# Where the maxima, the last queries' maxima and the weight steps stand in an attention pair

## The chip, the cores and the metric

The kernel runs on one core of a Trainium2 chip. The metric is the device time of one execution in microseconds (us). A core has TensorE (PE, matmuls; its weight loads are listed as PEld), VectorE (DVE), ScalarE (ACT), GpSimd (POOL), and SyncE (SP), which issues DMAs here. Matmuls write psum, which VectorE and ScalarE can read.

## The reference

Attention of 8 batches and 8 heads with 1152 keys of 64 dimensions, with the queries averaged in twos to 576, then a feed-forward step on the 4608 resulting tokens of 512 features:

```python
q_pool = q.reshape(B, H, S // 2, 2, D).mean(axis=3)
scores = scale * np.matmul(q_pool, k.transpose(0, 1, 3, 2))
scores = scores - np.max(scores, axis=-1, keepdims=True)
attn = np.exp(scores)
attn = attn / (np.sum(attn, axis=-1, keepdims=True) + 1e-09)
attn_out = np.matmul(attn, v)
x = attn_out.transpose(0, 2, 1, 3).reshape(B * S_pooled, H * D)     # 4608 x 512
h = x @ w_in                                                         # 512 x 2048
out = (h - np.tanh(h)) @ w_out                                       # 2048 x 512
```

All is float32. The row maximum is subtracted before the exponential, so it is needed before the first score tile can be finished.

## The kernel before

**Pairs.** Two heads make a pair; there are 32 pairs (`n_pair`), done one after the other, and after them the feed-forward stage (nine chunks of 512 tokens), which the change does not touch. Within a pair the two heads take the two halves of TensorE's rows, so most matmuls come in twos that start together.

**Three phases of a pair.** `scores` runs for 18 places (`NS`: two halves of 288 queries, nine key tiles of 128 each): eight matmuls (high by high, high by low, low by high, and the negative maxima `m_row` through `sel`) into one psum tile, then an exponential on ScalarE to `p`. GpSimd adds the nine `p` of a half in threes (`add_p`, 12 additions a pair). The value products follow, 18 places of four-column-group matmuls `p` by `v` into `o`, copied out by ScalarE after each half (`pv_out`). `sums` then multiplies GpSimd's sums with ones, which gives the softmax's denominators.

**Maxima.** The maxima of a pair are computed one pair ahead. `max_part(pi, i)` is a unit: for i under 12 two matmuls of 128 queries by 384 keys (high parts only), for i = 12 and 13 the last 64 queries (three matmuls for both units); each has a VectorE reduction to `mx`. `max_row` takes the maximum of `mx`, transposes it and sends it through DRAM into `m_row`.

**The ring.** All psum tiles of the attention stage come from one ring of four (`psum()`), in the order of the program: score tiles, maxima units, `o`, the ones products. A slot is free again when its reader has read it: the exponential, the reduction, or a copy on ScalarE.

**Inputs ahead.** For the pair two further on, at place `NS` (the first place of the value products), `query_sums` adds the two halves of the queries on VectorE and `high` makes rounded copies on ScalarE; at `NS` + 9 `minus_high` makes the negated copy, at `NS` + 16 `low` issues GpSimd's accumulating DMA. `load` (at `NS` + 12) fetches K and Q for the pair three further on; `reciprocals` (VectorE, `NS` + 10) come in every fourth pair.

**Weight steps.** The feed-forward weights are split into high and low parts in the background: 16 blocks of six steps, `begin` (ScalarE), `clamp` (three VectorE operations), `mid`, `high` (also loads the next block), one mask, `low` (also stores the block). Four steps are popped in each pair from pair 2 on, so they last until pair 25.

**Order.** Each engine's order is the order of the program: `InOrder` chains every instruction to the one before on its engine, so all have the line of that helper (L37). Instructions of one engine do not overtake each other; the places are fixed in the table `at`, which `run(pi, place)` empties. A maxima unit for the next pair follows the score tiles with place 1 and 2 of every three; the last queries' units stand behind the ones products.

Of the kernel before, what the change touches and what calls it, by code (L numbers as in the profile page):

```python
# [46 lines left out]
def attention_ffn_kernel(  # L47
# [117 lines left out]
    def hidden(s):  # L165

        mm = [(w, x, c) for w, x in ((0, s.x.h), (0, s.x.l), (1, s.x.h)) for c in range(NP)]
        for k in s.parts:
            for j, (w, x, c) in enumerate(mm):
                pe.matmul(s.h[:, k], wi[s.f][:, w, c], x[:, c, k], start=(j == 0), stop=(j == len(mm) - 1))  # L170
# [7 lines left out]
    def shrink(s, before):  # L178
        t = lambda name, dt=F32: gp.tile([P, 512], dt, name=name)
        all_ = t("g_u"), t("g_t"), t("g_s1"), t("g_s2"), t("g_m", mybir.dt.uint8), s.w  # L180
        s.s1 = all_[2]
        s.g_h = gp.tile([P, 512], F32R, name="g_hi", bufs=LAG + 1)
        s.g_l = gp.tile([P, 512], F32R, name="g_lo", bufs=LAG + 1)
        for k in s.parts:
            shrink_part(s, before, s.h[:, k], *(a[:, k] for a in all_))
            before = None
# [42 lines left out]
    with ExitStack() as actx:  # L229
# [27 lines left out]
        def psum():  # L257
            return ring.tile([P, 2, 512], F32, name="ps")
# [93 lines left out]
        def scores(w, half, kt):  # L352

            ks = slice(SQ + kt * P, SQ + (kt + 1) * P)
            qs = slice(half * HQ, (half + 1) * HQ)
            ps = psum()
            mm = [(w.hi[:, ks], w.hi[:, qs]), (w.hi[:, ks], w.lo[:, qs]), (w.lo[:, ks], w.hi[:, qs]), (sel, w.m[:, qs])]
            for i, (a, b) in enumerate(mm):
                for h in range(2):
                    pe.matmul(ps[:, h, 0:HQ], rows(a, h), rows(b, h), start=(i == 0), stop=(i == 3), skip_group_check=True)  # L360
            p = ppool.tile([P, 2, HQ], F32, name=f"p{kt}")
            act.activation(p, ps[:, :, 0:HQ], AF.Exp, scale=1.0 / 16)
            return p

        def tiled(out, lhs, rhs, i, **kw):
            n = lhs.shape[1]
            pe.matmul(out[i * n:i * n + n], lhs, rhs, skip_group_check=True, tile_position=(0, i * n), **kw)

        def add_p(ps, half, kt):

            k, r = divmod(kt, 3)
            if r == 1:
                ps.sum.append(sp_pool.tile([P, 2, HQ], F32, name=f"sum{half}_{k}"))
                pool.tensor_tensor(ps.sum[k], ps[kt - 1], ps[kt], op=ALU.add)
            elif r == 2:
                pool.tensor_tensor(ps.sum[k], ps.sum[k], ps[kt], op=ALU.add)

        def pv_out(w, half, o):
            if half == 0:
                w.o = op.tile([P, SQ], F32, name="o_s")  # L380
            act.activation(w.o[:, half * HQ:(half + 1) * HQ], o[:, 0, 0:HQ], AF.Copy)
            if half == 1:
                sp.dma_start(x_dram[w.hp, :, w.b * SQ:(w.b + 1) * SQ], w.o)

        def sums(w, ps_p):

            ps = psum()
            for i in range(3):
                for h in range(2):
                    for half in range(2):  # L390
                        tiled(ps[:, 0, 0:HQ], ones, ps_p[half].sum[i][:, h], 2 * h + half, start=(i == 0), stop=(i == 2))
            s = op.tile([P, HQ], F32, name="s_s")
            act.activation(s, ps[:, 0, 0:HQ], AF.Copy)
            sp.dma_start(s_dram[w.b, w.hp].rearrange("h (a n) -> (h a) n", a=2), s[0:P:32])
# [74 lines left out]
        work = []  # L469
# [6 lines left out]
        NS = 2 * KT  # L476

        def add(pi, place, f, *args):
            at.setdefault((pi, place), []).append(lambda: f(*args))

        for pi in range(1, n_pair):
            for i in range(12):
                add(pi - 1, i // 2 * 3 + 1 + i % 2, max_part, pi, i)
            if pi >= 2:
                for i in range(12, 14):
                    add(pi - 2, 2 * NS, max_part, pi, i)
            add(pi - 1, NS - 1, max_row, pi)
        for pi in range(n_pair):
            if pi >= 2:
# [54 lines left out]
        def run(pi, place):  # L544
            while at.get((pi, place)):
                at[pi, place].pop(0)()
# [3 lines left out]
        for pi in range(n_pair):  # L550
            w = pairs[pi]
            ps = [Half(), Half()]
            for place in range(NS):
                half, kt = divmod(place, KT)
                ps[half].append(scores(w, half, kt))
                add_p(ps[half], half, kt)
                run(pi, place)
            n = pi + EARLY - n_pair
            if n == 0:
                c = Chunk(0)  # L560
                steps = [Step(x0[0], f, c) for f in range(NF)]
            if n >= 0:
                hw = psum()
                steps[n].h, steps[n].w = hw[:, 0], hw[:, 1]
                hidden(steps[n])
            for place in range(NS):
                half, kt = divmod(place, KT)
                if place == 1 and n >= 0:
                    shrink(steps[n], steps[n - 1] if n else None)
                if kt == 0:  # L570
                    o = psum()
                for h in range(2):
                    tiled(o[:, 0, 0:HQ], w.v[:, kt, h], ps[half][kt][:, h], h, start=(kt == 0), stop=(kt == KT - 1))
                if kt == KT - 1:
                    pv_out(w, half, o)
                run(pi, NS + place)
                if pi >= 2 and place in (3, 6, 11, 15) and work:
                    work.pop(0)()
            sums(w, ps)
            run(pi, 2 * NS)  # L580
        assert not work and not any(at.values()), (len(work), [a for a in at if at[a]])


# [95 lines left out]
```

## Time and profile before

| | us |
|---|---|
| median of 3 runs | 1605.51 (1605.28 to 1606.35) |
| the profiled execution | 1605.09 |
| its span, first to last instruction | 1603.3 |
| one pair, from value products to value products | 24.10 |
| PE / DVE / ACT / POOL busy | 1575.0 / 1202.0 / 988.1 / 1120.2 |
| granted TensorE clock | 0.998 |

A row of a timeline has the start and the length in us, the engine, the line, the operation, the output and inputs by the program's names, the shape, how often it follows itself, and in brackets the engine's idle time before it and what ended it. Neighbours of one kind are merged, so `x4` can be two maxima matmuls and the first two of a score tile, which bear the same names (`ps<-kq_h`) and differ by their 384 or 288 columns. A row of the table of stretches has the stretch, its length, each engine's busy time and instructions in the order PE, PEld, DVE, ACT, POOL, the clock, the DMA share and GB/s. Matmul ends are modelled; their starts are not. `mx<-ps` is the reduction of a maxima unit, `p<-ps` an exponential, `w_t`, `w_hl`, `w_raw` and `w_off` belong to the weight steps, `rec` to the reciprocals, `raw<-q` is the query sum.

### The profile page before, as it was taken

How to read it: one execution, taken by the hardware profiler on the slowest of the kernel's cores; microseconds unless marked ns; L12 is line 12 of the kernel's file. 1: busy time of each engine (PE TensorE's matmuls, PEld its weight loads, DVE VectorE, ACT ScalarE, POOL GpSimd, SP SyncE). 2: the span in 40 equal slices, each digit the busy share in tenths (PEclk: the TensorE clock that was granted, in tenths of full speed). 3: DMA queues.
4: the chain of work that ended last, by engine and by line, in shares of the span. 5: the costliest groups of instructions: out<-in, count | busy, mean ns of one | idle time of the engine just before them, and what ended most of it. 6: DMA issues, size and time to landing. Idle time of an engine off the chain costs nothing.

```text
span 1603.3 us, 30786 instructions
## 1 busy us (share of the span) xinstructions
PE 1575.0 (98%) x12012; PEld 1221.9 (76%) x12012; DVE 1202.0 (75%) x1590; ACT 988.1 (62%) x1615; POOL 1120.2 (70%) x780
## 2 busy tenths in 40 slices
PE   5999999999999999999998999999999999999998
PEld 4777677777777777677777888888888888888886
DVE  6588788897888888775347777777777777777776
ACT  4676677676676676676635556555655655565654
POOL 3787787787787787786846676666757676766654
PEclk9999999999999999999999999999999999999999
DMA  5547767658576768564180101010010202020000
GB/s 173 173 145 205 227 201 230 209 181 275 155 245 200 236 204 263 166 204 122 50 330 20 66 14 67 9 55 23 8 66 14 66 14 66 14 67 14 27 1 27
DMA packets 84068, 193.59 MB, mean 121 GB/s; under 512 B 12370, under 2 KB 38994, under 8 KB 81874
## 3 DMA queue, kind: packets, MB, share of 16 engines
q1 hardware_dynamic: 79458, 164.20, 29.2%
q0 software_dynamic: 4464, 27.43, 8.8%
q8 instruction: 94, 1.54, 0.4%
q14 instruction: 52, 0.43, 0.1%
HBM read 126.12 MB, written 38.04 MB: 102 GB/s over the span
## 4 chain that ended last, share of the span: by engine, by line
PE 93%; DMA 3%; DVE 2%; ACT 1%; issue 0%; SPq 0%; POOLq 0%; POOL 0%; DVEq 0%; ACTq 0%
PE ps L37 47%; PE ps_h L37 23%; PE ps_o L37 23%; DMA w<-wo_dram 2%; DVE mx L37 1%; DMA s_dram<-s_s 0%; DMA rec<-s_dram 0%; DMA x_r<-r_dram 0%; DMA q<-in_q_dram 0%; ACT p L37 0%; DVE ps_w L37 0%; SPq L37 0%; ACT kq_h L37 0%; DVE w_t L37 0%; DVE kq_l L37 0%
## 5 line engine op out<-in xcount | busy, mean ns | idle before, releaser
L37 DVE TENSOR_REDUCE mx<-ps 128x2 f32<-128x768 f32 x448 | 395.5, 925 | 109.5 <-PE ps L37 109.3
L37 ACT ACTIVATE p<-ps 128x576 f32<-128x576 f32 x576 | 353.4, 653 | 84.7 <-PE ps L37 57.7
L37 POOL TENSOR_SCALAR g_m<-g_u 128x512 uint8<-128x512 f32 (+1 forms) x145 | 251.7, 1736 | 194.4 <-ACT g_u L37 181.3
L37 POOL TENSOR_TENSOR sum<-p,p 128x576 f32<-128x576 f32 x192 | 281.4, 1466 | 138.1 <-ACT p L37 138.1
L37 POOL TENSOR_TENSOR sum<-sum,p 128x576 f32<-128x576 f32 x192 | 298.6, 1555 | 15.6 <-ACT p L37 0.6
L37 PE MATMUL ps<-kq_h 64*128 64x288 f32 (+1 forms) x1920 | 284.7, 341 | 10.0 <-ACT kq_h L37 7.6
L37 PE MATMUL ps<-p,v 128*64 128x288 f32 x2304 | 286.4, 407 | 0.0
L37 PEld LDWEIGHTS ps<-p,v 128*64 128x64 f32 x2304 | 162.7, 137 | 114.6 <-ACT p L37 6.1
L37 POOL TENSOR_TENSOR g_lo<-g_s,g_hi 128x512 fp32r<-128x512 f32 (+1 forms) x145 | 186.9, 1289 | 84.7 <-ACT g_hi L37 84.7
L37 PE MATMUL ps_o<-w,g_hi 128*128 128x512 f32 x792 | 244.7, 390 | 1.0 <-ACT g_hi L37 1.0
L37 ACT ACTIVATE g_u<-ps_h 128x512 f32<-128x512 f32 (+1 forms) x142 | 84.1, 592 | 239.6 <-PE ps_h L37 237.9
L37 PEld LDWEIGHTS ps<-kq_h 64*128 64x128 f32 x1920 | 180.5, 185 | 58.7 <-ACT p L37 20.9
L37 PE MATMUL ps_h<-x_h,w 128*128 128x512 f32 (+1 forms) x800 | 216.0, 392 | 4.4 <-DVE g_t L37 4.4
L37 DVE SCALAR_TENSOR_TENSOR ps_w<-g_u,ps_h 128x512 f32<-128x512 f32 (+1 forms) x142 | 98.3, 693 | 162.1 <-ACT g_t L37 161.9
L37 ACT ACTIVATE g_s<-g_u,pc 128x512 f32<-128x512 f32 x290 | 193.2, 714 | 11.3
L37 PEld LDWEIGHTS ps_h<-x_h,w 128*128 128x128 f32 x800 | 150.3, 189 | 37.5 <-DVE g_t L37 4.9
L37 PEld LDWEIGHTS ps_o<-w,g_hi 128*128 128x128 f32 x792 | 148.5, 188 | 33.4 <-ACT g_hi L37 1.4
L37 PE MATMUL ps<-kq_h,kq_l 64*128 64x288 f32 x1152 | 170.3, 292 | 0.0
L37 PE MATMUL ps<-kq_l,kq_h 64*128 64x288 f32 x1152 | 170.3, 292 | 0.0
L37 PE MATMUL ps<-m_row,sel 64*128 64x288 f32 x1152 | 169.5, 291 | 0.0
L37 PE MATMUL ps_o<-w,g_lo 128*128 128x512 f32 x396 | 154.8, 391 | 0.6 <-POOL g_lo L37 0.5
L37 DVE COPY_PREDICATED g_s<-g_m,g_t 128x512 f32<-128x512 uint8 (+1 forms) x145 | 110.0, 758 | 17.0 <-POOL g_m L37 2.1
(112 smaller groups left out, 2359.2 us busy)
## 6 DMA issues: line engine op xcount, KB each, us to landing
kq_l<-raw POOLq DMA_DIRECT2D x31, 864.0 KB, 10.6
raw<-in_k_dram SPq DMA_DIRECT2D x32, 576.0 KB
q<-in_q_dram SPq DMA_DIRECT2D x32, 576.0 KB
v<-in_v_dram SPq DMA_DIRECT2D x32, 576.0 KB
x_dram<-o_s SPq DMA_DIRECT2D x32, 288.0 KB
x_l<-x_dram SPq DMA_DIRECT2D x9, 1024.0 KB
out_dram<-o_f SPq DMA_DIRECT2D x36, 256.0 KB
w_raw<-in_w_in_dram SPq DMA_DIRECT2D x8, 1024.0 KB
```

Source lines behind the costliest of these rows:

```text
L37: i = f(*args, **kwargs)
```

## The change

Three things move; no instruction is added or removed. A place of -1 is new: it runs before a pair's first score tile.

- Maxima units 0 and 1 run at place -1, units 2 to 9 after places 1, 3, ... 15, units 10 and 11 both after place 17, the last. Before, unit i ran after place `i // 2 * 3 + 1 + i % 2`: 1, 2, 4, 5, ... 16, 17.
- Units 12 and 13 run after the last value product (`2 * NS - 1`) and so ahead of `sums`, instead of behind it.
- Weight steps are popped at value places 0, 2, 4 and 6 and ahead of what `run` does there, instead of at 3, 6, 11 and 15 and behind it.

```diff
         for pi in range(1, n_pair):
             for i in range(12):
-                add(pi - 1, i // 2 * 3 + 1 + i % 2, max_part, pi, i)
+                add(pi - 1, min(max(2 * i - 3, -1), NS - 1), max_part, pi, i)
             if pi >= 2:
                 for i in range(12, 14):
-                    add(pi - 2, 2 * NS, max_part, pi, i)
+                    add(pi - 2, 2 * NS - 1, max_part, pi, i)
             add(pi - 1, NS - 1, max_row, pi)
@@
             ps = [Half(), Half()]
+            run(pi, -1)
             for place in range(NS):
@@
                 if kt == KT - 1:
                     pv_out(w, half, o)
+                if pi >= 2 and place in (0, 2, 4, 6) and work:
+                    work.pop(0)()
                 run(pi, NS + place)
-                if pi >= 2 and place in (3, 6, 11, 15) and work:
-                    work.pop(0)()
             sums(w, ps)
-            run(pi, 2 * NS)
```

## The prediction

> **What bounds the kernel now.** I read the page first, then a table of four stretches of one pair each, then the timelines of TensorE, its weight loads, VectorE, ScalarE and GpSimd over one pair.
>
> ```profile
> span 1603.3 us, 30786 instructions
> ...
> PE 93%; DMA 3%; DVE 2%; ACT 1%; issue 0%; SPq 0%; POOLq 0%; POOL 0%; DVEq 0%; ACTq 0%
> ```
>
> ```profile
> 402.67:426.77 24.10, 24.10 (x270) 17.78 (x268) 20.21 (x24) 17.18 (x27) 19.39 (x14) 1.00 0.62 173
> 426.77:450.86 24.09, 24.09 (x270) 17.76 (x268) 21.64 (x25) 16.01 (x26) 19.68 (x14) 1.00 0.68 203
> 669.15:693.25 24.10, 24.10 (x269) 17.74 (x267) 16.38 (x21) 16.41 (x26) 18.59 (x14) 1.00 0.47 138
> ```
>
> TensorE holds the chain, and a pair of heads takes 24.10 us whether VectorE is busy 21.6 us of it (weight steps) or 16.4 us (none). So today no weight step reaches the chain. "Busy" hides short stalls, because matmul ends are modelled; starts do not. Times below count from 402.67 (T), the start of this pair's value products, and from 411.55 (Z = T + 8.88), where they give way to the next kind of matmul.
>
> ```profile
> 402.67 8.95 PE L37 MATMUL ps<-p,v 128*64 128x288 f32 x72
> 411.55 1.66 PE L37 MATMUL ps<-sum,ones 128*32 128x288 f32 x24
> 413.14 0.79 PE L37 MATMUL ps<-kq_h,q_last 128*128 128x384 f32 x3
> 413.86 0.40 PE L37 MATMUL ps<-kq_h 64*128 64x288 f32 x2
> ...
> 415.02 0.65 PE L37 MATMUL ps<-kq_h 64*128 64x384 f32 x4
> ...
> 421.45 0.51 PE L37 MATMUL ps<-kq_h 64*128 64x384 f32 x4
> ...
> 422.21 0.62 PE L37 MATMUL ps<-kq_h 64*128 64x384 f32 x4
> ...
> 423.06 0.30 PE L37 MATMUL ps<-kq_h 64*128 64x288 f32 x2
> ...
> 423.60 0.51 PE L37 MATMUL ps<-kq_h 64*128 64x384 f32 x4
> ...
> 426.50 0.34 PE L37 MATMUL ps<-kq_h 64*128 64x384 f32 x2
> 426.77 0.46 PE L37 MATMUL ps<-p,v 128*64 128x288 f32 x2
> ```
>
> ```profile
> 415.26 0.19 PEld L37 LDWEIGHTS ps<-kq_h 64*128 64x128 f32 x2 [0.19 <-DVE mx L37]
> ...
> 422.43 0.19 PEld L37 LDWEIGHTS ps<-kq_h 64*128 64x128 f32 x2 [0.17 <-ACT p L37]
> ```
>
> A score tile alone takes 0.54 us (423.06 to 423.60), a maxima unit with a tile 0.76 (421.45 to 422.21) or, with the wait at 422.43, 0.85 (422.21 to 423.06). Three tiles and two units repeat every 2.15 us; without that wait 2.03 to 2.06. The wait is the psum ring: four slots handed out in turn, so each tile or unit needs the slot of the fourth allocation before it. At 422.43 that is a tile whose exponential ended just then; at 415.26, the third tile, it is the last-query unit, whose VectorE reduction ended just then. From 415.26 to the next value products is 11.51 us.
>
> **The score phase.** Now the order is two units, then (two tiles, one unit) eight times, two tiles, two units. Per two tiles and a unit the rows give 0.76 + 0.54 = 1.30, of which the 0.76 still contains a few hundredths of waiting. The loop through the reduction is near that:
>
> ```profile
> 402.03 1.82 DVE L37 TENSOR_REDUCE mx<-ps 128x2 f32<-128x768 f32 x2 [0.33 <-PE ps L37]
> ...
> 404.39 1.13 DVE L37 TENSOR_TENSOR raw<-q 128x576 f32<-128x576 f32 x1
> 405.45 1.90 DVE L37 TENSOR_SCALAR w_t<-w_hl 128x1024 int32<-128x1024 int32 x1
> 407.39 2.32 DVE L37 SCALAR_TENSOR_TENSOR w_hl<-w_hl,w_t 128x1024 fp32r<-128x1024 int32 x1
> 410.94 2.15 DVE L37 TENSOR_SCALAR w_t<-w_t 128x1024 f32<-128x1024 f32 x3 [1.23 <-ACT w_t L37]
> 413.79 1.42 DVE L37 TENSOR_REDUCE mx<-ps 128x2 f32<-128x768 f32 x2 [0.70 <-PE ps L37]
> ...
> 421.83 1.82 DVE L37 TENSOR_REDUCE mx<-ps 128x2 f32<-128x768 f32 x2 [0.33 <-PE ps L37]
> ```
>
> A unit at 421.45 is reduced from 421.83 (0.38 later); two reductions take 1.82, one 0.96; the slot is used 0.05 after. 0.38 + 0.96 + 0.05 = 1.39 after a unit the next pair of tiles may load weights, wanted about 1.28 to 1.38 after it. I take 1.29. From the third tile on: 0.63 (a tile after a wait, 422.43 to 423.06) + 0.54 + 7 x 1.29 + 0.17 + 0.27 (the two last units, 426.50 to 426.77 the one) = 10.64 us, instead of 11.51: **0.87 us less**.
>
> **The front of it.** Moving the last queries' three matmuls ahead of the ones products changes no TensorE work: 0.72 (413.14 to 413.86) + 1.59 (411.55 to 413.14) in either order, 2.31 after Z. Then the two new units, at Z + 2.31 and Z + 2.48, and two tiles. The slots: the third tile now needs the second front unit's slot. Its reduction ends 0.38 + 1.82 after Z + 2.31, so the third tile loads at Z + 4.56; today it does at 415.26 = Z + 3.71. **0.85 us more**. TensorE could have been there at 2.31 + 0.17 + 0.17 + 0.57 + 0.53 + 0.18 = Z + 3.93, so 0.63 of this is a new stall. Where VectorE is free, the two parts cancel: 8.88 + 4.56 + 10.64 = 24.08 us, 0.02 below 24.10.
>
> **VectorE in front of it.** Four reductions (last-query pair, two front units) must now be through before the third tile, and they stand behind the weight steps. If VectorE's weight work ends E after Z, they end E + 0.79 + 0.46 + 0.87 + 0.95 (back to back, from 1.42 and 1.82 a pair) and the third tile comes at Z + E + 3.12. It is late from E = 1.44 on, and a pair costs E - 1.46 more than today. Today the first of them is wanted only at 413.79 = Z + 2.24, and only one gates the tile. So what covered the weight steps shrinks by most of a microsecond. In front of them also comes more: both last units now end the phase, so the two reductions end at T + 1.77 (first unit 0.44 before T, 0.38, 1.82) instead of 403.85 = T + 1.18, and all VectorE work up to the next idle time shifts by 0.59.
>
> ```profile
> 405.56 1.64 ACT L37 ACTIVATE kq_h<-raw 128x1728 fp32r<-128x1728 f32 x1 [2.25 <-DVE raw L37]
> ...
> 409.74 1.17 ACT L37 ACTIVATE w_t<-w_raw 128x1024 f32<-128x1024 f32 x1
> ```
>
> ```profile
> 403.51 1.40 POOL L37 TENSOR_TENSOR sum<-p,p 128x576 f32<-128x576 f32 x1
> 404.99 1.81 POOL L37 TENSOR_TENSOR sum<-sum,p 128x576 f32<-128x576 f32 x1
> ...
> 416.04 1.43 POOL L37 TENSOR_TENSOR sum<-p,p 128x576 f32<-128x576 f32 x1 [4.24 <-ACT p L37]
> ```
>
> ```profile
> 457.03 2.83 DVE L37 TENSOR_SCALAR w_t<-w_t 128x1024 f32<-128x1024 f32 x3 [3.31 <-ACT w_t L37]
> ...
> 460.44 1.20 DVE L37 SCALAR_TENSOR_TENSOR w_hl<-w_raw,w_t 128x1024 int32<-128x1024 int32 x1
> ```
>
> ```profile
> 431.38 2.43 DVE L37 SCALAR_TENSOR_TENSOR w_hl<-w_raw,w_t 128x1024 int32<-128x1024 int32 x1
> 433.73 1.38 DVE L37 TENSOR_SCALAR rec<-rec 128x36 f32<-128x36 f32 x1
> 435.14 0.38 DVE L37 RECIPROCAL rec<-rec 128x36 f32<-128x36 f32 x1
> ...
> 436.14 1.22 DVE L37 SCALAR_TENSOR_TENSOR w_hl<-w_hl,w_t 128x1024 fp32r<-128x1024 int32 x1
> ```
>
> The six steps of a block fall four to a pair, so the pairs 2 to 25 come in three kinds, eight of each. The engines run their queues in order, and a step starts when its inputs are there, so other places change only what a step stands ahead of: VectorE's query sum, and ScalarE's copies.
>
> - Kind A (mask, low, begin, clamp; the pair at 402.67). Mask, query sum and low are the same three in another order and end at 409.71 + 0.59 = T + 7.63. Then ScalarE's begin (1.17) and the three clamp operations (2.15), with 0.05 at each hand-over: T + 11.0, E = 2.16. Cost 0.70. Begin now stands ahead of the half's output copy and the minus-high copy (about 1.65, as 405.56); the ring wants the second output copy only at Z + 2.3, so I put that at nothing, at most 0.3.
> - Kind B (mid, high, mask, low; at 426.77). Its last step ends at 437.36 = T + 10.59, with the reciprocals' two operations in front, of which the first (1.38) is mostly a wait; without them about 0.55 less. 10.04 + 0.59: E = 1.8. Cost 0.34.
> - Kind C (begin, clamp, mid, high; at 450.86). VectorE idled 3.31 here, because begin stood behind the high copies. Now begin is ahead of them; the clamp starts after the query sum at T + 3.4. But there GpSimd is still summing, and beside it one such operation takes 1.90 (405.45) instead of 2.15 / 3 = 0.72. 3.4 + 3 x 1.90 + 0.73 + 1.20 = T + 11.0: E = 2.1. Cost 0.64.
>
> Six of the 24 (every fourth pair from 4 on) also hold the reciprocals, 0.55 each that was covered until Z + 2.24. Sum: 8 x (0.70 + 0.34 + 0.64) + 6 x 0.55 - 6 x 0.02 (pairs without weight steps) = 13.4 + 3.3 - 0.1 = **+16.6 us**. The profiled execution took 1605.09 (0.42 below the median 1605.51): 1605.1 + 16.6 = 1621.7, so **1622**.
>
> On kind C one page speaks against the change more strongly than my row. A row shows 1.90 for an operation of 0.72 beside a sum of 1.40. The Trainium skill, "SBUF — State Buffer", Who interferes with whom, holds that the two engines share a port pair under an exclusive lock for a whole instruction, and the second one "fully blocks"; an operation could then wait out a whole sum, 0.72 + 1.40 = 2.12. By the row kind C costs 0.64, by the rule 3 x 0.22 = 0.66 more, and the sum would be 1627.
>
> **Bounds of what I can't see.** E: at best nothing shifts and kind C uses its idle time (E at or under 1.46 everywhere, total -0.6 us); at worst GpSimd's sums, which now start closer to the value products, block one more operation in each kind (+0.5 each, +12 us). The two last units at the end: the value products' first slot is a tile two allocations further back whose exponential has 0.9 us; taken as nothing, at most 0.2 a pair. SyncE: the block's stores and loads now go out ahead of the next K and Q loads.
>
> ```profile
> 437.11 8.89 SPq L37 DMA_DIRECT2D wi_dram<-w_hl  x2
> ```
>
> ```profile
> 446.00:456.00 10.00, 10.00 (x108) 7.29 (x106) 7.00 (x10) 7.04 (x12) 9.77 (x7) 1.00 0.94 319
> ```
>
> Behind such a store the K and Q loads (1.18 MB, 3.7 us at 319 GB/s) go out near 446 instead of before it, and VectorE wants them at 450.86 + 2.3 = 453.2. Some 3 us are left: taken as nothing, at worst 2 us in each kind-B pair. GpSimd's DMA waits for the minus-high copy, up to 2 us later in kind A; the 4.24 us idle at 416.04 hide it.
>
> **Rivals.**
> - *VectorE is in time.* The weight steps, popped earlier, are through by Z + 1.46, as kind C's idle 3.31 allows and kind B (24.09 us, 21.64 busy) speaks against. Then 30 pairs gain 0.02: 1604.5; not slower, no change. 20%.
> - *The third tile does not wait.* If the ring gives it another slot than the second front unit's, the 0.63 stall goes, with VectorE in time 30 x 0.69 (0.06 after the wait too): 1604.5 - 20.7 = 1584. Against it: 415.26 waits for exactly the allocation four back. 12%.
> - *The reduction loop closes each period.* Where weights must be loaded 0.11 before I allow, each of 8 periods stalls 0.11: 30 x 0.88 = 26 us on top, 1648; alone 1631. 10%.
>
> **How the numbers follow.** My forecast has 58%. 0.2% is 3.2 us, about what can be told from no change. Low end: 1604.5 less some 3 for the small terms, 1601; high end: 1622 + 12 (E at worst), 1634; outside are the second rival and most of the third. Faster: 12% and 6% of the first rival's edge. Same: 14% of the first rival and 3% of my forecast's low edge. Slower: the other 65%.
>
> **What would show it.** In the changed profile: a weight load of the third tile idle "<-DVE mx" in every pair (right), near 0.6 us where no weight step runs and 1 to 1.5 where one does; no "<-ACT p" waits of weight loads in mid-phase, a period of 1.29; pairs after 669 still 24.1 us, pairs of kinds A and C 24.6 to 24.9. It is wrong if the weight pairs stay at 24.1 (VectorE in time), if all pairs shrink to 23.4 (no front stall), or if waits of GpSimd or DMA show at the pair's border.

## The result, and the profile after

The changed kernel took 1619.81 us (median; 1619.41 to 1620.13), the kernel before 1606.35 beside it (1605.28 to 1606.93): a ratio of 1.0086, with a 95% interval of 1.0074 to 1.0097. It is 13.5 us slower; the forecast was 1622.

From the page of the changed kernel, the span and the shares of the chain of waits:

```profile
span 1617.9 us, 30798 instructions
...
PE 70%; DVE 20%; DMA 6%; issue 1%; SPq 1%; ACT 1%; DVEq 0%; POOLq 0%; POOL 0%; ACTq 0%
```

TensorE had 93% of the chain. Now a fifth of it runs through VectorE, whose busy time grew by 22 us (1202.0 to 1224.4). The table of stretches of the changed kernel, one pair to a row (stretch, length, busy time of PE, PEld, DVE, ACT, POOL, clock, DMA share, GB/s), shows where:

```profile
707.43:731.59 24.16, 23.74 (x270) 17.89 (x268) 16.73 (x21) 16.07 (x27) 18.85 (x14) 1.00 0.75 243
483.44:508.12 24.68, 24.18 (x269) 17.83 (x267) 20.34 (x24) 16.50 (x27) 19.42 (x13) 1.00 0.65 190
508.12:532.50 24.38, 24.12 (x269) 17.86 (x268) 21.29 (x23) 15.42 (x25) 19.43 (x13) 1.00 0.68 191
458.69:483.44 24.75, 24.19 (x269) 17.84 (x267) 20.33 (x24) 16.63 (x27) 18.55 (x13) 1.00 0.75 244
310.56:334.90 24.34, 24.08 (x269) 17.82 (x268) 21.22 (x24) 16.73 (x27) 19.27 (x13) 1.00 0.74 244
```

In this order: a pair without weight steps, kind A, kind B, and two of kind C. Kind C comes in two lengths, which the prediction did not have, and pairs 24 and 25 are longest of all (26.24 and 25.85). The next table takes the starts of the value products of all pairs in both traces and adds up pair lengths; its sum is the whole difference up to pair 31.

| pairs | before | after | more | forecast |
|---|---|---|---|---|
| 0, 1, 26, 27 (no weight steps) | 96.42 | 96.64 | +0.22 | -0.1 |
| kind A, 3 to 21 (7) | 169.29 | 173.23 | +3.9 | +5.5 |
| kind B, 4 to 22 (7) | 168.70 | 171.59 | +2.9 | +3.5 |
| kind C, 2 to 23 (8) | 192.85 | 197.53 | +4.7 | +6.2 |
| 24 (A, reciprocals) | 25.18 | 26.24 | +1.1 | +1.3 |
| 25 (B) | 24.34 | 25.85 | +1.5 | +0.3 |
| 28 to 30 | 77.54 | 77.47 | -0.1 | 0 |
| sum | 754.32 | 768.55 | +14.2 | +16.6 |

(The forecast column regroups the prediction's own terms: the 0.55 of the reciprocals is in pairs 12, 4 and 16, 8 and 20, and 24.) The traced executions differ by 14.9, somewhat more than the medians.

The timeline of TensorE and of its weight loads in the changed kernel, in the pair from 707.43, which has no weight step (Z = 716.32):

```profile
716.32 0.79 PE L37 MATMUL ps<-kq_h,q_last 128*128 128x384 f32 x3
...
718.63 0.76 PE L37 MATMUL ps<-kq_h 64*128 64x384 f32 x6
...
720.99 0.40 PE L37 MATMUL ps<-kq_h 64*128 64x288 f32 x2 [0.42 <-DVE mx L37]
...
722.15 0.47 PE L37 MATMUL ps<-kq_h 64*128 64x384 f32 x4
...
731.07 0.59 PE L37 MATMUL ps<-kq_h 64*128 64x384 f32 x4
```

```profile
720.99 0.19 PEld L37 LDWEIGHTS ps<-kq_h 64*128 64x128 f32 x2 [0.68 <-DVE mx L37]
```

The first front unit starts 2.31 after Z, the third tile loads at Z + 4.67 after 0.68 of waiting for a reduction, and 10.60 later the next value products start. From 722.15 to 731.07 lie seven units, 1.27 us each with their two tiles, with no such wait between them. In a pair with weight steps the reductions come later, and the wait spreads over the second front unit, the first tile and the third; the weight loads of the pair of kind A from 483.44:

```profile
495.32 0.18 PEld L37 LDWEIGHTS ps<-kq_h 64*128 64x128 f32 x2 [0.50 <-DVE mx L37]
495.79 0.19 PEld L37 LDWEIGHTS ps<-kq_h 64*128 64x128 f32 x2 [0.28 <-DVE mx L37]
...
497.52 0.19 PEld L37 LDWEIGHTS ps<-kq_h 64*128 64x128 f32 x2 [0.51 <-DVE mx L37]
```

Together they are 1.29, against the one wait of 0.68 without weight steps. The totals of the waits, before and then after, tell the same: those of weight loads on exponentials have shrunk to a fifth, those on reductions have grown threefold, and VectorE waits for a load of Q seven times instead of once.

```profile
PEld ps L37 <- ACT p L37: 27.5, 149, 0.4
...
PEld ps L37 <- DVE mx L37: 14.1, 40, 2.7
```

```profile
PEld ps L37 <- DVE mx L37: 42.1, 86, 2.7
...
DVE raw L37 <- DMA q<-in_q_dram: 10.8, 7, 4.5
...
PEld ps L37 <- ACT p L37: 5.9, 32, 0.2
```

(us in all, times, longest.)

### The profile page after: what moved, and what is told of

It is laid out like the page before. It is cut to its first block, busy times and chain, and to the rows that moved or that the text cites. A ratio compares the mean times of both kernels' runs of the same rounds, so it can differ in the third digit from the quotient of the medians.

```text
span 1617.9 us, 30798 instructions
## 1 busy us (share of the span) xinstructions
PE 1572.6 (97%) x12012; PEld 1224.7 (76%) x12012; DVE 1224.4 (76%) x1590; ACT 974.4 (60%) x1615; POOL 1121.1 (69%) x780
## 4 chain that ended last, share of the span: by engine, by line
PE 70%; DVE 20%; DMA 6%; issue 1%; SPq 1%; ACT 1%; DVEq 0%; POOLq 0%; POOL 0%; ACTq 0%
PE ps L37 24%; PE ps_h L37 23%; PE ps_o L37 23%; DVE mx L37 8%; DVE w_hl L37 4%; DVE w_t L37 4%; DMA q<-in_q_dram 4%; DVE raw L37 3%; DMA w<-wo_dram 2%; SPq L37 1%; ACT w_t L37 1%; DMA rec<-s_dram 0%; DVE nm L37 0%; DVE rec L37 0%; DVE ps_w L37 0%
## 5 line engine op out<-in xcount | busy, mean ns | idle before, releaser
L37 DVE TENSOR_REDUCE mx<-ps 128x2 f32<-128x768 f32 x448 | 400.8, 924 | 123.6 <-PE ps L37 123.6
L37 ACT ACTIVATE p<-ps 128x576 f32<-128x576 f32 x576 | 343.1, 652 | 77.9 <-PE ps L37 60.5
L37 POOL TENSOR_SCALAR g_m<-g_u 128x512 uint8<-128x512 f32 (+1 forms) x145 | 247.2, 1705 | 193.7 <-ACT g_u L37 180.9
L37 POOL TENSOR_TENSOR sum<-p,p 128x576 f32<-128x576 f32 x192 | 286.2, 1491 | 125.4 <-ACT p L37 125.4
L37 ACT ACTIVATE kq_h<-raw 128x1728 fp32r<-128x1728 f32 (+2 forms) x33 | 52.8, 1601 | 136.9 <-DVE raw L37 134.6
```

The lines of the kernel that those rows point to most:

```text
L37: i = f(*args, **kwargs)
```

## The experiments

Each ratio is against the kernel before, run beside it, with its 95% interval. E is, as in the prediction, the end of VectorE's weight work after Z.

**The three parts, each alone on the kernel before.** First only the new places of the twelve maxima units:

```diff
-                add(pi - 1, i // 2 * 3 + 1 + i % 2, max_part, pi, i)
+                add(pi - 1, min(max(2 * i - 3, -1), NS - 1), max_part, pi, i)
...
+            run(pi, -1)
```

> The kernel before with the maxima units' new places alone; the last queries' units stay behind the ones products, the weight steps at their old places. Theory (third tile waits for the reduction of the second front unit): now four reductions start only after the ones products. The last-query pair is reduced from Z + 2.24, the two front units from Z + 3.57, the second ends at Z + 5.4, so the third tile comes at Z + 5.5 instead of Z + 4.67 as measured in the changed kernel: a pair without weight steps takes 24.16 + 0.83 = 25.0 us, and nearly all 30 pairs alike, since VectorE's weight work (old places, 0.59 later) ends before Z + 2.24 but for kind C (0.25 late): 1606.3 + 30 x 0.9 + 2 = 1635. Rival (weight steps alone make the loss, the front of the score phase costs nothing): 1606 to 1608.

Measured: 1621.03 us, ratio 1.0095 (1.0081 to 1.0109). This alone costs as much as the whole change, but not in the way that was expected: a pair without weight steps takes 24.50, not 25.0, and kinds A and B take 24.49 to 24.61, kind C without reciprocals 24.54 to 24.63. The last queries' reductions now come behind the ones products, and the weight loads and VectorE of the pair from 683.65 show who waits:

```profile
695.79 0.19 PEld L37 LDWEIGHTS ps<-kq_h 64*128 64x128 f32 x2 [0.65 <-DVE mx L37]
...
697.12 0.46 PEld L37 LDWEIGHTS ps<-kq_h 64*128 64x128 f32 x4 [0.24 <-DVE mx L37]
```

```profile
694.78 4.01 DVE L37 TENSOR_REDUCE mx<-ps 128x2 f32<-128x768 f32 x5 [4.14 <-PE ps L37]
```

It is the first tile that waits (0.65), for a last-query reduction. With the prediction's reduction times (0.79 + 0.46 + 0.87 + 0.95) the second front unit is read at 694.78 + 3.07 = 697.85, but the third tile is in the merged row at 697.12 (a unit and a tile), and so loads before that. It did not take the slot four allocations back. In the compiled program's psum addresses it has the first tile's, whose exponential was over; in all other kernels here the slots do go in turn, up to pair 28. The expectation's step that failed is "third tile waits for the reduction of the second front unit".

Next only the last queries:

```diff
-                    add(pi - 2, 2 * NS, max_part, pi, i)
+                    add(pi - 2, 2 * NS - 1, max_part, pi, i)
...
-            run(pi, 2 * NS)
```

> The kernel before with the last queries' units ahead of the ones products, alone. Theory: the third tile's slot is then the ones products', long copied out; it comes at Z + 3.58 instead of Z + 3.71 and without the 0.06 to 0.1 after a wait: a pair without weight steps takes 23.9 to 23.95 us. The second tile now waits for the first last-query reduction, wanted for weight work that ends by Z + 1.8; kinds A (1.54) and B (1.23) do, kind C (1.90) loses 0.1, pairs with reciprocals some 0.4. 30 x -0.17 + 8 x 0.1 + 6 x 0.3 = -2.5 us: 1603.5 to 1604. Rival (VectorE gates every pair as soon as its reductions are wanted ahead of the ones products): slower than before, 1610.

Measured: 1607.41 us, ratio 1.0008 (0.9999 to 1.0017); nothing gained, where 1603.5 to 1604 were expected. A free pair takes 24.12. The third tile no longer waits, but the tile after it does; the weight loads of the free pair from 671.25:

```profile
684.58 0.19 PEld L37 LDWEIGHTS ps<-kq_h 64*128 64x128 f32 x2 [0.21 <-ACT p L37]
```

The wait moved from a reduction to an exponential. I read this so: with units in pairs in mid-phase ScalarE's exponentials pace the phase, and an earlier third tile meets them sooner.

Third only the places of the weight steps:

```diff
+                if pi >= 2 and place in (0, 2, 4, 6) and work:
+                    work.pop(0)()
                 run(pi, NS + place)
-                if pi >= 2 and place in (3, 6, 11, 15) and work:
-                    work.pop(0)()
```

> The kernel before with the weight steps' new places alone. Theory: VectorE's reductions are wanted only at Z + 2.24, and the weight steps end by Z + 2.1 without the 0.59 that the two last units add; nothing is gated: pairs 24.1 us, 1606 within 1.5 us. The query sum of some kind-C pairs waits for the K and Q loads behind the weight DMAs, covered too. Rival (the steps' new order by itself delays the pairs, by ScalarE's copies or the loads): kinds A and C 24.4 or more, 1611 or more.

Measured: 1605.48 us, ratio 0.9998 (0.9989 to 1.0007). Nearly all pairs take 24.10. E is 1.5 in kind A, 1.2 in B, 1.6 in C: the weight work ends late enough to gate the changed front, but the old front covers it.

**The change with the weight steps where they were.** The edit undoes the third part.

> The changed kernel with the weight steps back at their old places; maxima and last queries as changed. Theory (a pair loses E - 1.46 through VectorE, E now from the kernel before's ends plus 0.59): kind A 1.54 + 0.59 = 2.13, B 1.23 + 0.59 = 1.82, C 1.90 + 0.59 = 2.49, so A 24.8, B 24.45, C 25.1; the new places had helped kind C. But the K and Q loads and the x copies at the pairs 24 and 25 stand as before, about 1 us less there. 8 x 0.35 - 2 = 1 us more than the changed kernel: 1620 to 1622. Rival (the new places cause the loss): 1606 to 1608.

Measured: 1623.63 us, ratio 1.0115 (1.0099 to 1.0130), a little beyond what was expected. Kinds A and B are mostly within 0.1 of the changed kernel; kind C without reciprocals takes 25.05 to 25.08 (E 2.45 to 2.49), pair 2, the first with steps, 24.83. So the new places help kind C, as the prediction had it (begin ahead of the high copies), and their help is hidden in the kernel before.

**Less VectorE work.** In the changed kernel the three clamp operations and the mask are left out, so the weights are not split rightly:

```diff
-                    ts(f(self.t), f(self.t), lo_b, hi_b, op0=ALU.max, op1=ALU.min)
-                    ts(self.t, self.t, 0x08000000, 3, op0=ALU.bitwise_xor, op1=ALU.logical_shift_left)
-                    ts(self.t, self.t, 0x7FFFFFFF, None, op0=ALU.bitwise_and)
+                    pass
...
-                    lambda: ts(self.t, self.hl[:, 0], -0x800000, None, op0=ALU.bitwise_and),
+                    lambda: None,
```

> The changed kernel without the clamp's three VectorE operations and the mask operation of each weight block; the weights are then not split rightly, all else is done. Theory: VectorE is through with the remaining weight work by Z + 1.4 in all kinds, so every pair falls back to the 24.16 us of the pairs without weight steps, with some 0.2 left where reciprocals stand and in the pairs 24 and 25, where ScalarE's x copies stand behind VectorE: 1606.3 + 30 x 0.06 + 1.5 = 1609 to 1610, 10 us less than the changed kernel. Rival (the front wait or the places of the maxima make the loss in every pair): 1618 to 1620.

Measured: 1606.40 us, ratio 1.0004 (0.9995 to 1.0013). All pairs of the three kinds take 24.15 to 24.22; only pair 25 is longer (25.03). The loss is the weight steps' lateness, nearly all of it. The front and the ring alone, in all 30 pairs, cost no more than can be told from nothing.

**One front unit instead of two, one last unit.** This was to test the prediction's "two last units" (both reductions behind the last place shift VectorE by 0.59):

```diff
-                add(pi - 1, min(max(2 * i - 3, -1), NS - 1), max_part, pi, i)
+                add(pi - 1, (-1, 1, 2, 4, 6, 7, 9, 11, 12, 14, 16, 17)[i], max_part, pi, i)
```

> The changed kernel with one unit ahead of the scores and one at the end: units after places -1, 1, 2, 4, 6, 7, 9, 11, 12, 14, 16, 17. Theory: the third tile waits for the first front unit, reduced by Z + 3.70, and TensorE comes at Z + 3.76: no front wait. In the phase four groups of three tiles with two units wait 0.12 each, as in the kernel before, where six did. A pair without weight steps: 8.88 + 3.76 + 10.67 + 0.48 = 23.8; weight work ends 0.59 earlier than in the changed kernel, E at most 1.6, and gates no pair without reciprocals (0.3 with). 30 x -0.3 + 6 x 0.3 + 2 (pairs 24, 25) = -5: 1600 to 1602. Rival (the exponentials' chain, not the front, paces the phase, as in the run with the last queries ahead alone): 24.05 to 24.1 a pair, 1605 or more.

Measured: 1607.94 us, ratio 1.0016 (1.0007 to 1.0025). The table of stretches, a free pair and one of kind A (kind B takes 23.9):

```profile
673.03:696.85 23.82, 23.82 (x270) 17.75 (x268) 17.28 (x21) 16.30 (x27) 18.85 (x14) 1.00 0.50 142
476.36:500.58 24.22, 24.09 (x269) 17.78 (x267) 20.64 (x24) 16.73 (x27) 19.41 (x14) 1.00 0.68 200
```

The whole missed (1600 to 1602 were expected), though the free pair came out at 23.82 where 23.8 was expected: this order of the units is worth 0.34 against the changed kernel where VectorE is free. Kind A did not follow. VectorE and GpSimd in that pair of kind A (T = 476.36):

```profile
475.72 1.82 DVE L37 TENSOR_REDUCE mx<-ps 128x2 f32<-128x768 f32 x2 [0.33 <-PE ps L37]
...
478.09 1.50 DVE L37 TENSOR_SCALAR w_t<-w_hl 128x1024 int32<-128x1024 int32 x1
479.51 1.96 DVE L37 TENSOR_TENSOR raw<-q 128x576 f32<-128x576 f32 x1
481.39 2.44 DVE L37 SCALAR_TENSOR_TENSOR w_hl<-w_hl,w_t 128x1024 fp32r<-128x1024 int32 x1
```

```profile
466.09 1.43 POOL L37 TENSOR_TENSOR sum<-p,p 128x576 f32<-128x576 f32 x1 [3.85 <-ACT p L37]
...
477.63 1.41 POOL L37 TENSOR_TENSOR sum<-p,p 128x576 f32<-128x576 f32 x1
```

And the same rows of the changed kernel (T = 483.44):

```profile
483.30 1.82 DVE L37 TENSOR_REDUCE mx<-ps 128x2 f32<-128x768 f32 x2 [0.29 <-PE ps L37]
...
485.66 1.10 DVE L37 TENSOR_SCALAR w_t<-w_hl 128x1024 int32<-128x1024 int32 x1
486.69 1.96 DVE L37 TENSOR_TENSOR raw<-q 128x576 f32<-128x576 f32 x1
488.57 2.44 DVE L37 SCALAR_TENSOR_TENSOR w_hl<-w_hl,w_t 128x1024 fp32r<-128x1024 int32 x1
492.25 2.15 DVE L37 TENSOR_SCALAR w_t<-w_t 128x1024 f32<-128x1024 f32 x3 [1.24 <-ACT w_t L37]
```

```profile
473.27 1.42 POOL L37 TENSOR_TENSOR sum<-p,p 128x576 f32<-128x576 f32 x1 [4.31 <-ACT p L37]
...
484.81 1.40 POOL L37 TENSOR_TENSOR sum<-p,p 128x576 f32<-128x576 f32 x1
```

Read three times from T: the end of the last reduction, the start of GpSimd's ninth addition, and the end of the last of mask, query sum and low.

| kernel | reduction ends | ninth addition starts | last of the three ends | the last two apart |
|---|---|---|---|---|
| before (pair from 402.67) | 1.18 | 0.84 | 7.04 | 6.20 |
| after | 1.68 | 1.37 | 7.57 | 6.20 |
| one front unit | 1.18 | 1.27 | 7.47 | 6.20 |

The weight work keeps its distance to the additions, to the hundredth, and not to the reductions. The same holds beyond these three: in all pairs of kind A from 3 to 21 of seven kernels (these three, the steps alone, the steps moved back, and two further on, with earlier loads and with both last units at the end) the distance is 6.18 to 6.21, while the ninth addition starts anywhere from T + 0.79 to T + 1.64. With the reduction 0.50 earlier than in the changed kernel, low ends only 0.10 earlier: the first operation merely takes longer (1.50 instead of 1.10) and ends, in both, 0.55 after the end of the ninth addition. The shift that the prediction put down to the two last units belongs to GpSimd.

**Half the additions.** The test of that: GpSimd leaves out the second addition of every three exponentials, six of a pair's twelve, so the denominators lack a third of their terms.

```diff
-            elif r == 2:
-                pool.tensor_tensor(ps.sum[k], ps.sum[k], ps[kt], op=ALU.add)
```

> The changed kernel without every third addition on GpSimd (six a pair instead of twelve), so the softmax's denominators lack a third of their terms; all else is done. Revised theory (VectorE's weight steps are late because each waits out one of GpSimd's additions, which now begin closer to the value products; the two last units have nothing to do with it, since with one unit at the end the weight work ended only 0.07 earlier): with the additions over before the value products, VectorE's weight work ends by Z + 1.2 in every kind and all pairs fall to 24.15 to 24.2, the pairs 24 and 25 to 25: 1606 to 1608. Rival (VectorE is late by its own work and by the 0.5 of the two last units): kinds A and B gain little, 24.5 and 24.3, 1613 or more.

Measured: 1605.84 us, ratio 0.9999 (0.9990 to 1.0008). Everything of the change is in this kernel but those additions, and its loss is gone. VectorE in the pair of kind A from 476.04:

```profile
475.90 1.82 DVE L37 TENSOR_REDUCE mx<-ps 128x2 f32<-128x768 f32 x2 [0.28 <-PE ps L37]
...
478.27 0.65 DVE L37 TENSOR_SCALAR w_t<-w_hl 128x1024 int32<-128x1024 int32 x1
478.84 0.75 DVE L37 TENSOR_TENSOR raw<-q 128x576 f32<-128x576 f32 x1
479.50 1.22 DVE L37 SCALAR_TENSOR_TENSOR w_hl<-w_hl,w_t 128x1024 fp32r<-128x1024 int32 x1
482.89 2.15 DVE L37 TENSOR_SCALAR w_t<-w_t 128x1024 f32<-128x1024 f32 x3 [2.17 <-ACT w_t L37]
```

The reductions end as late as in the changed kernel (T + 1.68), but mask, query sum and low take 2.62 together instead of 5.50, and E falls from 2.08 to 0.13. In kinds B and C the weight work even ends 2.2 and 2.1 before Z. All pairs up to 27 take 24.14 to 24.23, 24 and 25 too. So the cause is VectorE's weight work beside GpSimd's additions: there the three operations take 1.7 to 2.6 times as long as here. That the changed order moves the additions toward them is what the three times above show.

**The K and Q loads earlier.** The changed kernel with the loads issued at the second place of the value products, so ahead of the block's stores in SyncE's queue:

```diff
-                add(max(pi - 3, 0), NS + 12 if pi > 2 else 0, load, pi)
+                add(max(pi - 3, 0), NS + 1 if pi > 2 else 0, load, pi)
```

> The changed kernel with the loads of K and Q for the pair three further on issued at value place 1 instead of 12, so ahead of the weight blocks' stores and loads in SyncE's order. Theory: the kind-C pairs whose query sum waits 1.3 us for Q (5, 14, 17 and with reciprocals 8 and 20) fall to the 24.34 of the pairs 11 and 23, where it doesn't wait: 5 x -0.4 = -2 us, 1617.5 to 1618. Rival (the wait on Q is covered by GpSimd's sums anyway): 1619.8, kind C unchanged.

Measured: 1618.61 us, ratio 1.0083 (1.0070 to 1.0097). As a whole this can't be told from the changed kernel (1.0086), but in the trace the long pairs of kind C take 24.37 to 24.43, where the changed kernel has 24.72 to 24.76. What they had waited for, in the changed kernel, on SyncE's queue and on VectorE (T = 458.69):

```profile
442.33 6.64 SPq L37 DMA_DIRECT2D wi_dram<-w_hl  x2
449.07 6.22 SPq L37 DMA_DIRECT2D r_dram<-rec  x1
...
455.81 0.42 SPq L37 DMA_DIRECT2D q<-in_q_dram  x1
```

```profile
462.32 1.27 DVE L37 TENSOR_TENSOR raw<-q 128x576 f32<-128x576 f32 x1 [1.32 <-DMA q<-in_q_dram]
```

The block's loads, its store and here the reciprocals' store go out first. The two stores hold SyncE's queue for 12.9 us, the Q load is issued at 455.81, and VectorE's query sum, with all weight work behind it, waits 1.32 for it. In pair 13 the stores hold the queue for no more than 2.60, and Q for pair 14's query sum is issued 12.75 us ahead of its value products (371.67 and 384.42); the query sum still waits 0.72, with the DMA engines busy all the time (a stretch of pair 13):

```profile
376.00:381.00 5.00, 5.00 (x74) 4.79 (x72) 3.71 (x5) 4.70 (x8) 4.92 (x4) 1.00 1.02 257
```

There, I take it, Q stands behind the block's bytes: two loads and a store of 1 MB each are some 12 us at such a rate. One pair got longer (18: 24.90 instead of 24.68). Its ninth addition starts at T + 1.64 instead of T + 1.37, and the three operations again end 6.2 after it; why the additions came later there is open.

**One front unit, both last units at the end**, to tell whether two ends cost anything by themselves:

```diff
+                add(pi - 1, (-1, 1, 3, 5, 6, 8, 10, 11, 13, 15, 17, 17)[i], max_part, pi, i)
```

> The changed kernel with one unit ahead of the scores and two at the end: units after places -1, 1, 3, 5, 6, 8, 10, 11, 13, 15, 17, 17. Theory: no front wait, two groups of three tiles with two units: 8.88 + 3.76 + 10.67 + 0.24 = 23.6 a pair without weight steps. VectorE is as late as in the changed kernel (E 2.08, 1.76, 1.74 to 2.13) and the third tile follows E by 2.2: kinds A and C 24.1, B 23.75, reciprocals 0.5 more. 8 x (0 - 0.35 - 0.1) + 6 x 0.5 - 6 x 0.5 + 2 = -1.6: 1603 to 1606; the two last units cost what the two groups saved. Rival (the late reductions do not matter once the third tile waits for the first front unit): 23.6 in all kinds, 1592.

Measured: 1607.98 us, ratio 1.0016 (1.0007 to 1.0024). Free pairs 23.70, kind A mostly 24.20 to 24.24, B 23.91 to 23.97. The total is a little above what was expected, but no dearer than with one last unit, so the time of the last reductions does not matter, and the free pair is 0.40 below the kernel before. The weight pairs and 24 and 25 (25.76 and 25.50) take the gain back.

**Fewer additions with the whole sum.** On top of that kernel, the ninth exponential of each half goes to the ones products directly: ten additions a pair instead of twelve, four terms instead of three.

```diff
-            elif r == 2:
+            elif r == 2 and kt < KT - 1:
...
-            for i in range(3):
+            for i in range(4):
...
+                        a = ps_p[half].sum[i] if i < 3 else ps_p[half][KT - 1]
```

> The run with one unit in front and two at the end, and in each half the ninth exponential goes to the ones products by itself: ten GpSimd additions a pair instead of twelve, four more matmuls of the ones products. By the revised theory GpSimd is done some 3 us earlier and VectorE's weight work ends before Z + 1.4, so no pair is gated: 23.70 + 0.24 (four matmuls in four column groups, as the ones products' 0.24 each) = 23.95 in all kinds, the pairs 24 and 25 near 24.5: 1599 to 1601, faster than before. Rival (VectorE late by its own work): kinds A and C 24.2 + 0.24, 1610 or more.

Measured: 1608.77 us, ratio 1.0017 (1.0008 to 1.0026); a miss. As expected, weight steps cost nothing any more: nearly all pairs take 24.19, with and without them. But the new term costs 0.5, twice what was taken. TensorE there:

```profile
486.18 1.66 PE L37 MATMUL ps<-sum,ones 128*32 128x288 f32 x24
487.66 0.67 PE L37 MATMUL ps<-p,ones 128*32 128x288 f32 x8
```

The program's four products are eight matmuls in the trace (the twelve before them are 24), at 1.48 / 24 = 0.06 each.

On top of that kernel, weight steps from pair 0 on, so that they end with pair 23:

```diff
-                if pi >= 2 and place in (0, 2, 4, 6) and work:
+                if place in (0, 2, 4, 6) and work:
```

> The kernel with four terms of the ones products, with the weight steps from pair 0 instead of pair 2 on, so they are over before the pairs 24 and 25, where ScalarE's x copies stand behind VectorE. Theory: these two pairs fall to 23.95 to 24.1, the pairs 0 and 1 stay at 23.95: 0.5 to 1.5 us less than with the steps from pair 2. Rival (the first weight block's data arrive too late for pair 0, or the x copies are late by themselves): the same or slower.

Measured: 1607.97 us, ratio 1.0007 (0.9998 to 1.0016), 0.8 us less than with the steps from pair 2, as expected, though the two intervals overlap. Pairs 24 and 25 go from 24.98 and 24.33 to 24.20 and 24.19. Why these two are long, in the changed kernel's pair 25 (value products end at 666.30): TensorE, ScalarE, VectorE.

```profile
668.50 1.66 PE L37 MATMUL ps<-sum,ones 128*32 128x288 f32 x24 [1.40 <-ACT o_s L37]
```

```profile
667.42 0.63 ACT L37 ACTIVATE x_h<-x_r 128x512 fp32r<-128x512 f32 x1 [2.73 <-DVE x_r L37]
667.96 0.39 ACT L37 ACTIVATE o_s<-ps 128x288 f32<-128x288 f32 x1
```

```profile
666.71 0.68 DVE L37 TENSOR_TENSOR x_r<-x_l,x_r 128x512 f32<-128x512 f32 x1
```

VectorE's product for the feed-forward stage stands behind the weight steps, ScalarE's copy of it stands ahead of the output copy, and the ones products wait 1.40 for the slot that this output copy frees.

**Together.** One front unit with both last units at the end and all twelve additions, the loads at the second value place, and the steps from pair 0.

> The run with one unit in front and two at the end (twelve additions), the K and Q loads at value place 1, and the weight steps from pair 0 on. Theory: 23.70 a pair without weight steps, kinds A 24.2, B 23.95, C 23.95 (its query sum no longer waits for Q; 24.28 before), 0.45 more with reciprocals, no lost time in the pairs 24 and 25: 3.5 us less than the kernel before, 1602.5, at the edge of what can be told. Rival (the loads and the pairs 24 and 25 are not what made the run with one unit in front and two at the end slower than the sum of its pairs): 1606 to 1608.

Measured: 1600.98 us, ratio 0.9962 (0.9949 to 0.9974), so 5.8 us below the kernel before; the changed kernel, in a comparison of its own, is 13.5 above it. Its stretches: a free pair, and kinds A and C (the kinds fall on other pairs here; kind B is like C).

```profile
643.12:666.82 23.70, 23.70 (x270) 17.79 (x268) 16.93 (x21) 16.17 (x27) 18.83 (x13) 1.00 0.47 141
64.72:88.95 24.23, 23.98 (x270) 17.80 (x268) 20.32 (x24) 16.62 (x27) 19.41 (x13) 1.00 0.60 170
...
474.88:498.78 23.90, 23.90 (x270) 17.83 (x268) 21.22 (x24) 16.83 (x27) 19.27 (x14) 1.00 0.77 241
```

Kind C lost its Q wait (24.23 to 24.31 mostly, before these two edits), and pair 24 has no weight steps any more and takes 23.71, like a free pair. Kind A still costs 0.5 more than a free pair (0.7 in two pairs).

## Why the prediction was right, point by point

- **The forecast and its sign: right.** 1622 forecast, 1619.8 measured; of the +16.6 in terms the trace shows +14.2. "VectorE is in time" fell, since weight pairs did not stay at 24.1, and "the reduction loop closes each period" fell, since the period is 1.27.
- **The front: right.** The third tile was put at Z + 4.56 and came at Z + 4.67; the new stall was put at 0.63, and the weight load is idle for 0.68. **The score phase** was put at 10.64 from there and took 10.60. A free pair should have come to 24.08 and takes 24.16; the 0.08 is the 0.11 at the third tile less 0.04.
- **VectorE in front of it: right, with smaller sizes.** E was put at 2.16, 1.8 and 2.1 for kinds A, B and C, and is 2.08, 1.77 and 1.74, or 2.14 where Q is late. The cost, put at E - 1.46, is E - 1.50: 0.58, 0.28 and 0.24 or 0.65. The wait in a pair with weight steps, put at 1 to 1.5 at the third tile, is 1.29 in kind A, but spread over three loads. The reciprocals' 0.55 measures about 0.5 in pairs 12, 4 and 16. The kinds came to 3.6 us less than their terms: 1.4 in the three pairs of kind C without the wait for Q, 0.6 in pairs 3 and 6, which already took 24.38 before, the rest in the smaller E and reciprocals.
- **"both last units now end the phase, so ... all VectorE work up to the next idle time shifts by 0.59": the wrong cause with nearly the right size.** Low ended 0.53 later. The runs with one front unit and with half the additions put this down to GpSimd: its twelve additions follow each other from the first exponentials on, the first one started 10.73 ahead of the next value products (416.04 in the prediction's row) and now starts 10.17 ahead (473.27 to 483.44). So the additions stand 0.5 deeper in the stretch where the weight steps run. The new order alone does not give all of this: behind pairs without weight steps the first addition starts 10.42 ahead. The rest comes when weight work of the pair before holds back the first tiles, as in the three waits above. Pair 2, the first with steps, shows the difference: E is 1.52 there, and it takes 24.17. That 0.59 was near in size was luck. The prediction held the additions as "GpSimd's sums, which now start closer to the value products", but only as a bound.
- **Kind C's price: the mechanism and the row right, the sum a little high.** Where Q is in time (pairs 11 and 23) the clamp starts at T + 3.34 (put at 3.4), and VectorE's row in the pair from 310.56 has its three operations:

```profile
313.90 5.54 DVE L37 TENSOR_SCALAR w_t<-w_t 128x1024 f32<-128x1024 f32 x3
```

  They take 5.54 beside the additions, where the prediction put 3 x 1.90 = 5.70. With mid and high the work ends at T + 10.62 instead of 11.0; the larger part of the difference is in these terms, the rest in rows that overlap by some hundredths where they follow each other. In kind A the query sum takes 1.96 against 0.75 and low 2.44 against 1.22 alone, each longer by 1.2. By the Trainium skill's rule of an exclusive lock ("SBUF — State Buffer", Who interferes with whom) the operation that comes second waits out the other's whole instruction. As an estimate from that rule, a whole addition of 1.40 for each operation makes 6.36 for the clamp (3 x 2.12) and 1.40 more for each of query sum and low. The trace comes near this and stays under it.
- **"K and Q loads ... taken as nothing": wrong.** Five pairs of kind C wait for Q, about 0.4 each; the earlier load takes it away. The bound (2 us in a pair) held. Waits of DMA at the pair's border were one of the prediction's own signs of being wrong, and in this term it was: DMA has 6% of the chain instead of 3%. The bytes of the weight loads and the reciprocals' store were not in its sum of what now goes out first. Without this wait kind C would have been the cheapest kind instead of nearly the dearest: two errors that cancelled.
- **ScalarE's output copy, "nothing, at most 0.3": wrong in two pairs.** In 24 and 25 a copy for the feed-forward stage waits for VectorE ahead of it. The two cost 2.6 us more, where 1.6 was forecast for other reasons.
- **"The third tile does not wait": not so here**, but the run of the maxima places alone had just this, a ring that gives the third tile another slot, so the rival was not idle.
- **The moved last queries: right to be counted as no gain.** Alone they bring nothing, because the exponentials take over the wait.

What stays open: why the ring is not in turn in one program, why the additions of pair 18 come later with earlier loads, and what between VectorE and GpSimd makes their operations wait for each other; the runs show only the times.

## What to carry to other kernels

When an order is changed so that one phase gets shorter, ask which engine runs a fixed chain of work from that phase's beginning (here GpSimd's additions): its tail is pushed into the next phase, and what runs slower beside it (here VectorE's weight operations and query sum) is slowed there. Read an engine's lateness against several candidates, and trust the one whose distance stays the same in all kernels, as 6.2 us did here. And a cover has a size: weight work that ended 1.2 to 1.9 after Z cost nothing in front of one reduction wanted at Z + 2.24, and work that ended 1.7 to 2.1 after Z, in front of four reductions, cost most of the 13 us.

## What the runs showed of the hardware that was not expected

- VectorE operations from SBUF to SBUF (psum not involved) stretch beside GpSimd additions until they keep step with them: mask 0.65 to 1.10 or 1.50, query sum 0.75 to 1.96, low 1.22 to 2.44, while GpSimd's last addition of a pair of kind A takes 2.29 in both kernels (at 408.70 and 490.00) instead of 1.43. An earlier start is swallowed by a longer first operation. The reductions from psum do not: 0.96 each, in the score phase, beside additions of 1.43.
- A store of the weight block (two issues) held SyncE's queue 2.5 to 9 us (8.89 at 437.11 before, 6.64 at 442.33 after, 2.60 at 368.50), with the reciprocals' store 6.22 more at 449.07; a load behind them goes out that much later.
